# Windowed attention with a two-layer feed-forward: a list schedule, with and without 400 trial changes of its deadlines

## The chip, the cores and the metric

The kernel runs on one core of a Trainium2 chip. The metric is the device time of one execution in microseconds (us), lower is better; a profiled execution also has a span, from its first instruction to its last. The engines are TensorE (PE, its weight loads shown apart as PEld), VectorE (DVE), ScalarE (ACT), GpSimd (POOL) and SyncE (SP), which here issues every DMA of the kernel.

## The reference

```
q, k, v: [8, 8, 576, 64]                      # batch, heads, sequence, head size, float32
scores = q @ k.T / sqrt(64) + slope[h] * -|i - j|     # slope[h] = 2 ** -(h + 1)
scores = where((i >= j) & (i - j < 128), scores, -1e9)
x      = softmax(scores) @ v                  # reordered to [4608 tokens, 512]
h      = x @ w_in                             # [512, 2048]
g      = h if h >= 1; 0 if h <= -1; (h + 1) ** 2 / 4 between
out    = g @ w_out                            # [2048, 512] -> [4608, 512]
```

The weights arrive as float64 and are turned into float32 on the chip.

## The kernel before, in words

The 4608 tokens are cut into nine chunks of 512. Attention runs per chunk and head (72 heads in all, two of them a pair), in blocks of 128 queries against 256 keys: scores on TensorE (lines 667 to 674), the window and the bias on VectorE (680, 683), the exponential on ScalarE (687), a scaling by the sum (698), a turn of the block (on TensorE, line 760, for heads under 28, otherwise on VectorE and through memory), triangular masks on GpSimd (708, 711, 776, 779), and the product with the values (820). The first 16 heads work in plain float32; the later ones, like the feed-forward, split every operand into a high part in a rounded format and the rest of it, and take three products (high by high, high by rest, rest by high).

The first layer sweeps eight groups of the 2048 hidden units per chunk. Chunk 0 uses the plain blocks of w_in (A11, A12, A21, A22); chunks 1 to 8 use seven products of a Strassen form (line 883), named A11, A12, S2, S3, S1, S4 and A22 on the weight side. `build` splits such a weight block into a tile and stores it to memory (d_A, d_S, line 516); `fetch` brings it back for each later chunk (w_A, w_S, line 522) into a ring of ten places. The nonlinear step and its split are lines 894 to 903, the second layer lines 915 to 917, the copies of its sums lines 922 and 923, the stores of the result line 926.

During chunk 0 the float64 weights are loaded in 32 pieces of 512 KB (`fetch_raw`, tile raw, line 426) and turned into float32 (`convert`, ScalarE lines 451 and 461, VectorE lines 456 and 464). The raw pieces, the sixteen finished tiles of w_out, six tiles of w_in that come back from memory and one tile for turning blocks share NW = 17 places in SBUF (tag w). The tag o has two places, used in turn: for w_out on its way, for some weight sums that are being split, and for results on their way out.

All of this is not emitted in program order. Each operation is a `Node` of a `Plan` with the time that it costs on each engine that could do it; a DMA costs SP 0.4 us, then its bytes at 370 GB/s behind those before it, and lands 2.8 us or more after its issue. Each node also has a deadline (`late`). `forward` simulates the engines and lets each take, whenever it is free, the ready operation with the earliest deadline; `later` sets deadlines anew by walking that order backwards from its end. `schedule` does this twelve times, keeps the order with the earliest planned end, and the instructions are written in that order. On the chip each engine runs its own instructions strictly in that order, and semaphores hold it where an operand or a place is not ready.

Of the kernel before, what the change touches and what calls it, by code (L numbers as in the profile page):

```python
# [2 lines left out]

# [6 lines left out]
F32 = mybir.dt.float32  # L10
F32R = mybir.dt.float32r
# [18 lines left out]
PRODUCTS = (("A11", "B11"), ("A12", "B21"), ("S2", "T2"), ("S3", "T3"), ("S1", "T1"), ("S4", "B22"), ("A22", "T4"))  # L30
# [26 lines left out]
class Plan:  # L57


    CROSS, SAME, BACKLOG, STRETCH, SWAP, ROUNDS = 0.09, 0.04, 4.0, 2.0, 8.0, 12  # L60

    def __init__(self):
        self.nodes, self.slots, self.turn, self.common = [], {}, {}, {}
# [87 lines left out]

    def schedule(self, engines, bandwidth):
        self.deadlines()
        best = None
        for _ in range(self.ROUNDS):
            order = self.forward(engines, bandwidth)
            end = max(n.end for n in order)
            if best is None or end < best[0]:
                best = end, order, [(n, n.eng, n.start, n.end) for n in order], \
                    [(b, b.slot) for _, bufs in self.common.values() for b in bufs]  # L160
            self.later(order)
        for n, n.eng, n.start, n.end in best[2]:
            pass
        for b, b.slot in best[3]:
            pass
        return best[1]

    def forward(self, engines, bandwidth):
        free = {e: 0.0 for e in engines}
# [127 lines left out]
def windowed_attention_then_ffn(  # L297
# [9 lines left out]
    nc = tc.nc  # L307
# [3 lines left out]
    NT, DM = out.shape  # L311
    P = 128
    NPAIR = H // 2
    NCC = DM // P
    NFC = 16
    NG = NFC // 2
# [22 lines left out]
    def buf(pool, tag, n, shape, dtype, name):  # L339
        return plan.buf(pools[pool], tag, n, shape, dtype, name)  # L340
# [6 lines left out]
    def dve(n, f, port=False):  # L347
        return {"DVE": (n * 0.00104 + 0.068, n * 0.00104 + 0.155, f, port)}

    def dve_fast(n, f):  # L350
        return {"DVE": (n * 0.00052 + 0.070, n * 0.00052 + 0.160, f, True)}

    def act(n, f, extra=0.092):
        return {"ACT": (n * 0.00083 + extra, n * 0.00083 + extra + 0.105, f, False)}

    def act_ps(n, f):
        return act(n, f, 0.05)
# [13 lines left out]
    def pe(t, f):  # L371
        return {"PE": (t, t + 0.2, f, False)}

    def dma(nbytes, f):
        return {"SP": (0.4, 2.8, f, nbytes)}

    MM = {128: 0.112, 256: 0.1192, 512: 0.2305}

# [36 lines left out]
    wi32 = w_in.bitcast(I32)  # L415
    wo32 = w_out.bitcast(I32)
    WEIGHTS = [(g, n, f) for g in range(NG) for n in (0, 1) for f in (0, 1)]
    NW = 2 * NFC + 1 - NFC

    def fetch_raw(i):  # L420
        g, n, f = WEIGHTS[i]
        r = raw[i] = plan.shared(pools["wp"], "w", NW, [P, DM, 2], I32, f"raw_{i}", lambda free: (
            all(x.slot is not None for x in raws[:i]) and
            free > sum(x.slot is None for h, x in kept if h < g)))
        raws.append(r)
        plan.op(dma(P * DM * 8, lambda: DMA.dma_start(r.t.rearrange("p f w -> p (f w)"),
                                                      (wo32 if n else wi32)[f * NG + g])), (), [r])

    def convert(i):
        g, n, f = WEIGHTS[i]  # L430
        r = raw.pop(i)
        if n == 0:
            if f == 0:
                w_of[g] = buf("xp", ("T3", "T4", "T2")[g % 3], 1, [P, 2, DM], F32, f"w_{g}")
            w, key = w_of[g], f
        else:
            w, key = buf("fp", "o", 2, [P, DM], F32, f"fo_{g}_{f}"), None
            fo[g, f] = w

        def low():  # L440
            return r.t[..., 0]

        def high():
            return r.t[..., 1]

        def o():
            return (w.t if key is None else w.t[:, key]).bitcast(I32)

        def scale_high():
            if SIGN_BY_SLOPE:  # L450
                S.activation(high().bitcast(F32), high().bitcast(F32), AF.Prelu, scale=2.0 ** -112, alpha=2.0 ** 32)  # L451
            else:
                S.mul(high().bitcast(F32), high().bitcast(F32), 2.0 ** -112)

        def shift():
            V.tensor_scalar(o(), high(), 3, None, ALU.logical_shift_left)
            if not SIGN_BY_SLOPE:
                V.scalar_tensor_tensor(o(), high(), -0x80000000, o(), ALU.bitwise_and, ALU.bitwise_or)

        plan.op(act(DM, scale_high, 0.13), [(r, 1)], [(r, 1)])  # L460
        plan.op(act(DM, lambda: S.activation(low(), low().bitcast(U32), AF.Copy, scale=2.0 ** -29), 0.13),  # L461
                [(r, 0)], [(r, 0)])
        plan.op(dve_fast(DM, shift), [(r, 1)], [(w, key)])
        plan.op(dve(DM, lambda: V.tensor_tensor(o(), o(), low(), ALU.add), True), [(r, 0), (w, key)], [(w, key)])

    def split_out(g, f):

        o = fo.pop((g, f))
        w = wo_of[f * NG + g] = plan.shared(pools["wp"], "w", NW, [P, 2, DM], F32R, f"wo_{g}_{f}", lambda free: True)
        kept.append((g, w))  # L470
# [12 lines left out]
    def unspill(g):  # L483
        w = w_of[g] = plan.shared(pools["wp"], "w", NW, [P, 2, DM], F32, f"w32_{g}", lambda free: (
            all(x.slot is not None for _, x in kept)))
        unspilled.append(w)
        d = spilled.pop(g)
        plan.op(dma(P * DM * 8, lambda: DMA.dma_start(w.t, d.t)), [d], [w])

    def operand(g, name):  # L490

        if name[0] == "A":
            w, f = w_of[g], int(name[1]) - 1
            k0 = 0 if name[2] == "1" else 2
            return w, f, lambda: w.t[:, f, k0 * P:(k0 + 2) * P].rearrange("p (c f) -> p c f", c=2)
        if (g, name) not in sums_w:
            a, alu, b = dict(S1=("A21", ALU.add, "A22"), S2=("S1", ALU.subtract, "A11"),
                             S3=("A11", ALU.subtract, "A21"), S4=("A12", ALU.subtract, "S2"))[name]
            (ab, ak, af), (bb, bk, bf) = operand(g, a), operand(g, b)
            s = buf("fp", "sw", 4, [P, 2, P], F32, f"{name}_{g}")  # L500
            plan.op(dve(2 * P, lambda: V.tensor_tensor(s.t, af(), bf(), alu), True), [(ab, ak), (bb, bk)], [s])
            sums_w[g, name] = s
        s = sums_w[g, name]
        return s, None, lambda: s.t

    def build(g, name):
        b, key, f = operand(g, name)
        if name in PLAIN or g >= NG - LATE:
            t = buf("ring", "r", 10, [P, 2, 2, P], F32R, f"b_{g}_{name}")
        else:  # L510
            t = buf("fp", "o", 2, [P, 2, 2, P], F32R, f"b_{g}_{name}")
        plan.op(rounded(2 * P, lambda: t.t[:, 0], f), [(b, key)], [(t, 0)])
        plan.op(dve(2 * P, lambda: V.tensor_tensor(t.t[:, 1], f(), t.t[:, 0].bitcast(F32), ALU.subtract), True),
                [(b, key), (t, 0)], [(t, 1)])
        d = scratch[g, name] = plan.buf(dr, f"d_{g}_{name}", 1, [P, 4 * P], F32, f"d_{g}_{name}")
        plan.op(dma(P * 2048, lambda: DMA.dma_start(d.t, t.t.bitcast(F32).rearrange("p s c f -> p (s c f)"))), [t], [d])
        return t
# [201 lines left out]
    def turn_blocks(m, z):  # L719


        if not turned:
            turned.append(plan.shared(pools["wp"], "w", NW, [P, 2, 4 * P], F32, "turned", lambda free: (
                all(x.slot is not None for _, x in kept) and all(x.slot is not None for x in unspilled))))
# [181 lines left out]
    def layer2(c, n, fc, t):  # L906
        first, last = n == 0, n == NFC - 1
        if first and t == 0:
            accs[c] = [bank(f"acc{i // 2}", 2, f"acc_{c}_{i}") for i in range(SIZES[c])]
        a = accs[c][t]  # L910
        ts = slice(t * P, (t + 1) * P)
        w, (gh, gl) = wo_of[fc], gs[c, fc]

        def f():
            T.matmul(a.t, gh.t[:, ts], w.t[:, 0], start=first, stop=False)  # L915
            T.matmul(a.t, gh.t[:, ts], w.t[:, 1], start=False, stop=False)  # L916
            T.matmul(a.t, gl.t[:, ts], w.t[:, 0], start=False, stop=last)  # L917

        plan.op(pe(3 * MM[512], f), [gh, gl, w], [a])
        if last:  # L920
            o = buf("fp", "o", 2, [P, DM], F32, f"o_{c}_{t}")
            alts = act_ps(DM, lambda: S.copy(o.t, a.t))
            alts.update(dve(DM, lambda: V.tensor_copy(o.t, a.t)))  # L923
            plan.op(alts, [a], [o])
            r = (STARTS[c] + t) * P
            plan.op(dma(P * DM * 4, lambda: DMA.dma_start(out[r:r + P, :], o.t)), [o], ())
        if t == SIZES[c] - 1:
            del gs[c, fc]
# [22 lines left out]
    at = [0]  # L951
# [134 lines left out]
    for c in range(NCHUNK):  # L1086
        steps = sweep_steps(c)
        n = len(steps)
        now, end = ready[min(c + 1, NCHUNK)], ready[min(c + 2, NCHUNK)]
# [45 lines left out]
```

## Time and profile before

| what | value |
|---|---|
| median of three runs | 963.92 us (962.33 to 966.59) |
| profiled execution | 964.71 us, span 963.0 us |
| TensorE, VectorE, ScalarE, GpSimd busy | 99%, 90%, 69%, 23% of the span |
| granted TensorE clock | 1.000 |
| moved by DMA | 227.40 MB, mean 236 GB/s |

A busy share is the mean over stages with different limits. TensorE's matmuls are pipelined and their ends modelled, so a matmul is shown longer (0.39 us for 512 columns) than its distance from the next; how much TensorE really stands still is read from starts, waits and the chain of work.

### The profile page before, as it was taken

To read this page: it belongs to the slowest core of one execution; us is meant where nothing else is said; L and a number is where in the kernel's file an instruction comes from. 1 tells how busy PE (TensorE), PEld (TensorE's weight loads), DVE (VectorE), ACT (ScalarE), POOL (GpSimd) and SP (SyncE) were. 2 spreads that over 40 slices of the span, in tenths; PEclk is the share of its full clock that TensorE was granted. 3 is DMA by queue.
4 is the path that set the end of the run, shared out by engine and by line. 5 is a ranking of instruction groups with operands and counts; after the bars stand their busy time and mean duration, and the time that the engine had idled before them with its cause. 6 is when DMAs were issued, how large, how long until landed. Compare 5 with 4: busy or idle time off the path is not lost.

```text
span 963.0 us, 19573 instructions
## 1 busy us (share of the span) xinstructions
PE 951.1 (99%) x6320; PEld 863.4 (90%) x6320; DVE 869.9 (90%) x2183; ACT 661.4 (69%) x1657; POOL 218.5 (23%) x274
## 2 busy tenths in 40 slices
PE   8999999999999999999999999999999999999998
PEld 7889998999889998999899989899899999989987
DVE  6999999999999999999999999999999999984453
ACT  7998777877887677665876577667766777553322
POOL 2311111222331222322232212312232222210000
PEclk9999999999999999999999999999999999999999
DMA  9678886676867876887788869787888778766651
GB/s 345 235 244 276 300 269 204 229 220 222 246 204 255 253 243 211 284 259 245 223 278 254 255 212 279 244 255 223 257 276 251 218 233 272 225 174 201 174 152 44
DMA packets 133237, 227.40 MB, mean 236 GB/s; under 512 B 13712, under 2 KB 36240, under 8 KB 133136
## 3 DMA queue, kind: packets, MB, share of 16 engines
q1 hardware_dynamic: 133136, 226.15, 74.7%
q8 instruction: 51, 0.84, 0.3%
q14 instruction: 50, 0.41, 0.1%
HBM read 185.20 MB, written 40.89 MB: 235 GB/s over the span
## 4 chain that ended last, share of the span: by engine, by line
PE 83%; DVE 7%; ACT 6%; DMA 3%; issue 1%; POOL 0%; SPq 0%; ACTq 0%; DVEq 0%; POOLq 0%
PE hA L883 17%; PE hB L883 13%; PE acc L916 12%; PE acc L915 12%; PE acc L917 12%; PE x L820 6%; PE h L883 3%; PE s L673 2%; PE s L674 2%; ACT z L687 2%; PE s L671 1%; ACT raw L451 1%; DMA raw<-in_moe_w_out_dram 1%; PE p L760 1%; ACT raw L461 1%
## 5 line engine op out<-in xcount | busy, mean ns | idle before, releaser
L915 PE MATMUL acc<-wo,gh 128*128 128x512 f32 x576 | 228.0, 396 | 0.1
L916 PE MATMUL acc<-wo,gh 128*128 128x512 f32 x576 | 227.3, 395 | 0.0
L917 PE MATMUL acc<-wo,gl 128*128 128x512 f32 x576 | 225.7, 392 | 0.2
L708 POOL TENSOR_SCALAR_AFFINE_SELECT lu<-lu 128x512 fp32r<-128x512 f32 x112 | 100.6, 898 | 516.5 <-ACT lu L364 179.6
L1025 ACT COPY s<-hA 128x256 f32<-128x256 f32 x192 | 70.8, 369 | 98.7 <-PE hA L883 93.5
L687 ACT ACTIVATE z<-z,nmax 128x128 f32<-128x128 f32 x288 | 113.3, 395 | 26.9 <-DVE nmax L683 25.6
L917 PEld LDWEIGHTS acc<-wo,gl 128*128 128x128 f32 x576 | 108.2, 188 | 25.6 <-DVE gl L903 1.4
L915 PEld LDWEIGHTS acc<-wo,gh 128*128 128x128 f32 x576 | 108.9, 189 | 9.8 <-DVE o L923 0.3
L916 PEld LDWEIGHTS acc<-wo,gh 128*128 128x128 f32 x576 | 109.1, 189 | 8.8
L897 ACT ACTIVATE m<-m 128x512 f32<-128x512 f32 x144 | 90.6, 630 | 28.2 <-DVE m L894 26.3
L899 DVE SCALAR_TENSOR_TENSOR h<-h,m 128x512 f32<-128x512 f32 x128 | 95.0, 743 | 12.3 <-ACT m L897 11.7
L883 PEld LDWEIGHTS hA<-x_T,w_S 128*128 128x128 f32 x696 | 95.4, 190 | 8.7 <-ACT s L1025 3.1
L883 PE MATMUL hA<-x_T,w_S 128*128 128x256 f32 x696 | 102.2, 283 | 1.0 <-ACT s L1025 1.0
L1020 DVE TENSOR_TENSOR h<-hB,s 128x256 f32<-128x256 f32 x192 | 79.7, 415 | 24.8 <-PE hB L883 20.6
L903 DVE TENSOR_TENSOR gl<-h,gh 128x512 fp32r<-128x512 f32 x128 | 91.2, 713 | 1.9 <-ACT gh L364 0.7
L711 POOL TENSOR_SCALAR_AFFINE_SELECT lu<-lu 128x512 fp32r<-128x512 f32 x112 | 92.9, 851 | 0.0
L683 DVE CUSTOM_DVE_ANT_0 z<-s,rel 128x128 f32<-128x128 f32 x288 | 70.8, 282 | 0.5
L680 DVE COPY_PREDICATED s<-older,s 128x256 f32<-128x256 uint32 x144 | 59.8, 420 | 9.4 <-PE s L671 5.1
L364 ACT CAST gh<-h 128x512 fp32r<-128x512 f32 x75 | 46.5, 620 | 24.9 <-DVE h L899 24.0
L820 PE MATMUL x<-lu,vs 128*128 128x256 f32 (+3 forms) x560 | 62.8, 259 | 0.0
L820 PEld LDWEIGHTS x<-lu,vs 128*128 128x128 f32 (+1 forms) x560 | 57.4, 163 | 3.9 <-issue 0.2
L673 PE MATMUL s<-kk,ql 128*128 128x256 f32 x224 | 57.7, 281 | 1.0 <-DVE ql L598 0.7
(129 smaller groups left out, 2049.2 us busy)
## 6 DMA issues: line engine op xcount, KB each, us to landing
w_S<-d_S SPq DMA_DIRECT2D x232, 256.0 KB, 3.4
w_A<-d_A SPq DMA_DIRECT2D x192, 256.0 KB, 3.7
kr<-in_k_dram SPq DMA_DIRECT2D x112, 160.0 KB, 3.6
d_turn<-turned SPq DMA_DIRECT2D x44, 256.0 KB, 3.5
turned<-d_turn SPq DMA_DIRECT2D x44, 256.0 KB, 3.7
vn<-in_v_dram SPq DMA_DIRECT2D x33, 320.0 KB, 3.7
out_dram<-o SPq DMA_DIRECT2D x36, 256.0 KB, 4.1
qr<-in_q_dram SPq DMA_DIRECT2D x33, 256.0 KB, 4.2
```

The lines of the kernel that those rows point to most:

```text
L687: plan.op({"ACT": (0.385, 0.48, lambda i=i: S.activation(z.t[:, i], z.t[:, i], AF.Exp, bias=nmax.t[:, i:i + 1], scale=-1.0, accum_out=sm.t ...
L708: G.affine_select(out=lu[s].t[:, 0:2 * nb:2], in_=a.bitcast(F32), pattern=[[0, nb], [-1, P]], base=0, channel_multiplier=1, compare_op=ALU ...
L711: G.affine_select(out=a, in_=a.bitcast(F32), pattern=[[0, nb], [1, P]], base=0, channel_multiplier=-1, compare_op=ALU.is_ge, fill=0.0)
L820: T.matmul(px[:rows, q0 * P:q1 * P], sv, mv.rearrange("p a w -> p (a w)"), start=(w == 0), stop=(w == len(todo) - 1), skip_group_check=True)
L883: T.matmul(o.t[:, at:at + 2 * P], w.t[:, a, kb], x.t[:, b, kb], start=start and n == 0, stop=stop and n == len(todo) - 1, skip_group_check ...
L897: plan.op(act_fn(n, lambda: S.activation(m.t, m.t, AF.Square, scale=0.5)), [m], [m])
L899: plan.op(dve(n, lambda: V.scalar_tensor_tensor(f.t, h.t, 1.0, m.t, ALU.max, ALU.min), not psum), src + [m], dst)
L903: plan.op(dve(n, lambda: V.tensor_tensor(gl.t, f.t, gh.t.bitcast(F32), ALU.subtract), True), dst + [gh], [gl])
L915: T.matmul(a.t, gh.t[:, ts], w.t[:, 0], start=first, stop=False)
L916: T.matmul(a.t, gh.t[:, ts], w.t[:, 1], start=False, stop=False)
L917: T.matmul(a.t, gl.t[:, ts], w.t[:, 0], start=False, stop=last)
L1020: plan.op(dve(2 * P, lambda: V.tensor_tensor(f.t[:, key * 2 * P:(key + 1) * 2 * P], b.t[:, :2 * P], s.t, ALU.add)), [b, s], [(f, key)])
```

## The change

The plan tries 400 more orders behind the twelve rounds. Each takes the best order's deadlines, picks a stretch of the planned time (5, 20 or 60 us long; for even trials it begins in the first 0.3 of the span, for odd ones anywhere) and an engine, moves the deadlines of that engine's operations there by random amounts (each by its own, all of a kind by the same, or all by the same), simulates, and keeps the new order where its planned end is no later. The draws have a fixed seed. The number of places under tag w goes from 17 to 20, and that under tag o from two to four; the scratch reserved for DMAs that software issues is set to 1024. In the plan a raw load lands 4.3 us after its issue in place of 2.8. `build` no longer stores a block that none of the seven products uses (A21, eight tiles).

```diff
-    CROSS, SAME, BACKLOG, STRETCH, SWAP, ROUNDS = 0.09, 0.04, 4.0, 2.0, 8.0, 12
+    CROSS, SAME, BACKLOG, STRETCH, SWAP, ROUNDS, TRIALS = 0.09, 0.04, 4.0, 2.0, 8.0, 12, 400
...
-        best = None
-        for _ in range(self.ROUNDS):
+        best, draw = None, random.Random(1)
+        for trial in range(self.ROUNDS + self.TRIALS):
+            if trial >= self.ROUNDS:
+                self.shift(best, draw, trial)
+            late = {n: n.late for n in self.nodes}
             order = self.forward(engines, bandwidth)
             end = max(n.end for n in order)
-            if best is None or end < best[0]:
+            if best is None or end <= best[0]:
                 best = end, order, [(n, n.eng, n.start, n.end) for n in order], \
-                    [(b, b.slot) for _, bufs in self.common.values() for b in bufs]
-            self.later(order)
+                    [(b, b.slot) for _, bufs in self.common.values() for b in bufs], late
+            if trial < self.ROUNDS:
+                self.later(order)
...
+    def shift(self, best, draw, trial):
+
+        end, _, placed, _, late = best
+        for n in self.nodes:
+            n.late = late[n]
+        at, span = draw.uniform(0, end if trial % 2 else 0.3 * end), draw.choice((5, 20, 60))
+        by, kind, eng = draw.choice((0.3, 1.0, 3.0)), draw.randrange(3), draw.choice(("PE", "DVE", "DVE", "ACT", "ACT", "SP"))
+        alike, together = {}, draw.gauss(0, by)
+        for n, _, start, _ in placed:
+            if at <= start < at + span and next(iter(n.alts)) == eng:
+                if kind == 0:
+                    n.late += draw.gauss(0, by)
+                elif kind == 1:
+                    n.late += alike.setdefault(n.alts[eng][2].__code__, draw.gauss(0, by))
+                else:
+                    n.late += together
...
-        return {"SP": (0.4, 2.8, f, nbytes)}
+        return {"SP": (0.4, landing, f, nbytes)}        # landing=2.8, and 4.3 for raw loads
...
-    NW = 2 * NFC + 1 - NFC
+    NW = NFC + 4
...
-            w, key = buf("fp", "o", 2, [P, DM], F32, f"fo_{g}_{f}"), None
+            w, key = buf("fp", "o", 4, [P, DM], F32, f"fo_{g}_{f}"), None
...
+        if all(name != w for w, _ in PRODUCTS):
+            return t
         d = scratch[g, name] = plan.buf(dr, f"d_{g}_{name}", 1, [P, 4 * P], F32, f"d_{g}_{name}")
...
-    nc = bacc.Bacc("TRN2", target_bir_lowering=False, num_devices=1)
+    nc = bacc.Bacc("TRN2", target_bir_lowering=False, num_devices=1, dynamic_dma_scratch_size=1024)
```

More of the change, by code (lines that the diff above doesn't have):

```diff
@@ L1 @@
 import heapq
+import random
 from contextlib import ExitStack
@@ L372, in pe, with dma @@
         return {"PE": (t, t + 0.2, f, False)}
-    def dma(nbytes, f):
-        return {"SP": (0.4, 2.8, f, nbytes)}
+    def dma(nbytes, f, landing=2.8):
+        return {"SP": (0.4, landing, f, nbytes)}
     MM = {128: 0.112, 256: 0.1192, 512: 0.2305}
@@ L426, in fetch_raw @@
         plan.op(dma(P * DM * 8, lambda: DMA.dma_start(r.t.rearrange("p f w -> p (f w)"),
-                                                      (wo32 if n else wi32)[f * NG + g])), (), [r])
+                                                      (wo32 if n else wi32)[f * NG + g]), 4.3), (), [r])
     def convert(i):
@@ L510, in build @@
         else:
-            t = buf("fp", "o", 2, [P, 2, 2, P], F32R, f"b_{g}_{name}")
+            t = buf("fp", "o", 4, [P, 2, 2, P], F32R, f"b_{g}_{name}")
         plan.op(rounded(2 * P, lambda: t.t[:, 0], f), [(b, key)], [(t, 0)])
@@ L920, in layer2 @@
         if last:
-            o = buf("fp", "o", 2, [P, DM], F32, f"o_{c}_{t}")
+            o = buf("fp", "o", 4, [P, DM], F32, f"o_{c}_{t}")
             alts = act_ps(DM, lambda: S.copy(o.t, a.t))
```

## The prediction

> **What bounds the kernel now.** I read the page's busy times first, then the stretches, the chain of work in order of time, and last what TensorE waited for.
>
> ```profile
> span 963.0 us, 19573 instructions
> PE 951.1 (99%) x6320; PEld 863.4 (90%) x6320; DVE 869.9 (90%) x2183; ACT 661.4 (69%) x1657; POOL 218.5 (23%) x274
> ...
> 0.00:24.00 24.00, 21.38 (x122) 18.87 (x123) 16.42 (x82) 17.22 (x56) 6.01 (x25) 1.00 0.94 345
> 24.00:72.00 48.00, 44.73 (x321) 40.72 (x320) 45.84 (x149) 47.13 (x128) 11.84 (x16) 1.00 0.69 241
> 72.00:144.00 72.00, 72.00 (x481) 66.06 (x480) 69.54 (x176) 56.35 (x127) 9.67 (x10) 1.00 0.84 280
> 144.00:280.00 136.00, 134.50 (x916) 122.22 (x915) 132.54 (x350) 104.91 (x263) 33.85 (x40) 1.00 0.70 219
> 280.00:700.00 420.00, 419.19 (x2813) 380.99 (x2812) 404.95 (x985) 297.69 (x757) 114.83 (x132) 1.00 0.81 249
> 700.00:900.00 200.00, 200.00 (x1330) 182.15 (x1329) 173.31 (x393) 121.99 (x298) 42.34 (x52) 1.00 0.75 230
> 900.00:963.00 63.00, 59.32 (x351) 52.35 (x349) 27.26 (x53) 16.16 (x34) 0.00 (x0) 1.00 0.39 113
> ```
>
> The stretches give, after their length, busy us of PE, PEld, DVE, ACT, POOL, then the granted clock (1.00 throughout), the DMA share and GB/s. TensorE's idle time is 2.62, 3.27, 0, 1.50, 0.81, 0 and 3.68 us: nearly all lies in the first 72 us, between 144 and 280, and at the very end. A matmul's shown end is modelled, so busy time hides part of a stall. What the work takes by itself comes from the chain in order of time (start, us, what):
>
> ```profile
> 1.66 3.68 PE idle L1072 x16
> ...
> 64.98 1.43 PE h L883 x12
> 67.81 1.79 PE x L820 x16
> 71.03 0.86 PE s L671 x4
> 73.32 0.44 PE p L760 x4
> 161.39 0.12 PE s L674
> 163.99 0.97 PE x L820 x10
> 370.49 0.23 PE acc L915
> 371.19 0.23 PE acc L915
> 373.25 0.71 PE hB L883 x6
> ```
>
> and, from the timeline, the last matmul:
>
> ```profile
> 958.93 0.39 PE L917 MATMUL acc<-wo,gl 128*128 128x512 f32 x1
> ```
>
> The sum by these rates, counts from the code. The second layer has 9 chunks x 16 x 4 x 3 = 1728 matmuls; 370.49 to 371.19 is three of them (0.233 each), 371.19 to 373.25 nine (0.229); at 0.231 they take 399.2 us. 512 products of six at 0.715 (half of 1.43): 366.1. Values of 56 later heads at 0.965: 54.0; of the early heads, 8 with seven products and 8 with eight at 1.79/8: 26.9. Scores of later heads, 448 x 0.118: 52.9; of early heads, 32 groups at 0.86: 27.5. Transposes of 28 heads at 0.44: 12.3. The filler at the start 3.7. Together 942.6. Of the span of 963.0 this leaves 20.4: 1.7 before the first matmul, 3.8 behind the last (963.0 less 958.93 and 0.23), and about **14.9 us of stalls** strung through the run; the visible idle time without the two ends (11.88 less 1.66 and 3.68) is 6.5. So no order of this work is worth more than 15 us, and the visible part is 6.5.
>
> What TensorE's weight loads waited for in the first 72 us (total, times, longest):
>
> ```profile
> PEld s L671 <- DVE gh L774: 1.3, 1, 1.3
> PEld s L671 <- DVE xn L829: 1.3, 2, 1.0
> PEld s L671 <- ACT gh L773: 0.9, 2, 0.5
> PEld p L760 <- ACT z L687: 0.9, 2, 0.7
> PEld h L883 <- DVE x_B L854: 0.8, 1, 0.8
> PEld p L760 <- DVE z L698: 0.8, 1, 0.8
> ```
>
> With five smaller ones (0.6 to 0.2, together 2.1) and without the wait for the filler's operand at the start these are 8.1 us, and nearly every one is VectorE or ScalarE coming late with a piece of early attention: a question of order. From 24 to 72 us, VectorE is busy 45.84 and ScalarE 47.13 of 48 us, so both together have 3.0 us left there; only bringing forward what feeds more TensorE work can fill the gaps.
>
> **The change part by part.** *The trials.* They add no instruction. Even trials start their stretch in the first 0.3 of the planned end, odd ones anywhere, so about two thirds of 400 fall where the stalls are. Bounds: nothing (the planned end falls, the chip does not follow) and 8.1 us in the first 72. Durations there are steady (a group of scores 0.86, a transpose group 0.44), so a planned order can hold on the chip; but with 3.0 us of room on two engines I take less than half, 3.2 us. Behind 72 us the idle time that counts is 1.50 + 0.81 = 2.3, scattered; the plan sees perhaps a third of it, as it has no late landings: 0.8. Below nothing is possible too, since an order that the plan thinks tight has less to spare; I charge 0.3 for new stalls. If those gaps close, next in line is VectorE: 132.54 of 136 us from 144 to 280.
>
> *Buffers.* Twenty places of raw weights for 17, and four output buffers for two:
>
> ```profile
> raw<-in_moe_w_in_dram SPq DMA_DIRECT2D x16, 512.0 KB, 6.1
> raw<-in_moe_w_out_dram SPq DMA_DIRECT2D x16, 512.0 KB, 6.5
> ACT raw L451 <- DMA raw<-in_moe_w_in_dram: 2.7, 4, 1.0
> ACT raw L451 <- DMA raw<-in_moe_w_out_dram: 0.4, 1, 0.4
> ...
> ACT o L922 <- DMA out_dram<-o: 1.8, 2, 1.4
> PEld acc L915 <- DVE o L923: 0.3, 1, 0.3
> ```
>
> The whole price of late raw weights is 3.1 us on ScalarE, which stands idle 15.65 of 72 us in 72 to 144, and no row of TensorE names them there. The output buffers cost ScalarE 1.8 and TensorE 0.3. Bounds 0 and 3.4, both from these rows; the one TensorE row decides, so 0.2. Memory for them comes from the scratch of software-made DMAs, which this kernel does not issue: 0.
>
> *The longer landing* for raw loads (4.3 for 2.8 in the plan) moves them earlier in SP's order. With 512 KB at the plan's 370 GB/s (1.4 us) and 0.2, the plan expected 4.4 us and now expects 5.9, against 6.1 and 6.5 on the chip: nearer. Thirteen of the 32 loads are issued in or just behind the stretch where the DMA share is 0.94:
>
> ```profile
> 11.58 0.91 SPq L426 DMA_DIRECT2D raw<-in_moe_w_in_dram  x2
> ...
> 27.08 0.33 SPq L426 DMA_DIRECT2D raw<-in_moe_w_in_dram  x1
> ```
>
> Behind a raw load that goes early, the queries and keys wait 1.4 us of transfer each. Bounds +1.4 and -0.4 us; I take 0, as ScalarE is not late there on more than the 3.1 above. The Trainium skill, "DMA: Bandwidth & Descriptors", section "Anatomy of one DMA — SWDGE (gpsimd) path", fits 2.0 us plus bytes over 436 GB/s, an estimate of 3.2 us for 512 KB (its fit is for another path of issue); by it the loads were planned late enough before, the change only pulls them forward without need, and this term would be up to the +1.4. The rows disagree with it (6.1 and 6.5), so it gets no place in the sum.
>
> *Stores left out.* A21's eight split tiles are no longer written to memory:
>
> ```profile
> d_A<-b_A SPq DMA_DIRECT2D x32, 256.0 KB, 3.8
> L516 SPq DMA_DIRECT2D d_A<-b_A x32: 319/326/1617, 40.5 to 145.9; - x32
> ```
>
> Eight of the 32 stores go: 8 x 0.33 = 2.6 us of SP and 2.1 MB, and with each the wait for its tile at the head of SP's queue, which held back the fetches behind. No row shows TensorE waiting for a fetch, so that is 0 on the path (bounds 0 and 2.6); the room is cover for the raw loads.
>
> **Sum.** -3.2 -0.8 +0.3 -0.2 = -3.9 us. The profiled execution took 964.7 (span 963.0 and 1.7 around it), 0.8 above the median of the three runs, 963.9. So 960.8 against the profiled one and **960.0** on the median's scale. About 0.5% (4.8 us) is what a measurement of this kernel can tell from no change.
>
> **Rivals.** *A, the forecast:* a good part of the early stalls goes; 957 to 962.5. Chance 0.50.
>
> *B, the plan's gain is not the chip's:* the end improves in the plan, while the chip's remaining stalls (14.9 by the sum, of which only 8.1 stand in a place where order is plainly at fault) just move. For it: both engines that feed TensorE are nearly full from 24 to 280 us (VectorE 45.84 + 69.54 + 132.54 = 247.9 of 256). 962.5 to 966; chance 0.23.
>
> *C, most stalls go:* 8.1 at the start and 2.3 later: 963.9 - 10.4 = 953.5; 950 to 957. For it: 400 trials that never give back a gain, two thirds of them on the first 0.3. Against it: the first heads' path from load through scores, exponential, transpose and values has to be run through once before there is other work, and the 3.0 us of room. Chance 0.20.
>
> *D, slower:* fetched weights become late. The order chosen for the plan's end lets fetches of w_A and w_S come just in time by a fixed landing, while
>
> ```profile
> w_A<-d_A SPq DMA_DIRECT2D x192, 256.0 KB, 3.7
> DMA to landing us min/median/max: 2.0/3.7/7.0
> ```
>
> (last row: of all transfers from and to d_A). One at the long end is 7.0 - 3.7 = 3.3 us late, TensorE runs in order, and nothing covers it. One such fetch eats most of the gain; from three on (9.9 against 4.2 gained) the kernel is over 5 us slower, about 969. Against it: no row of TensorE's waits today names a fetch. 966 to 972; chance 0.07.
>
> **How the numbers follow.** Faster by over 0.5% means under 959.1: all of C and (959.1 - 957)/5.5 = 0.38 of A, 0.20 + 0.19 = 0.39. Slower by over 0.5% is over 968.7: most of D, 0.05. The rest, 0.56, is no change. The range 955.5 to 965.0 leaves out some 0.09 of C, 0.04 of B and all of D, 0.20; the likeliest case's own range is 957 to 962.5.
>
> **What would show it.** Right: TensorE's idle time from 0 to 72 us falls from 5.9 to about 3.5, the weight loads' waits there from 8.1 to about 5; the stretch from 280 to 900 us stays as it is; raw's waits on ScalarE and o's on TensorE vanish with the time hardly touched; d_A has 24 stores. Wrong: the early waits keep their total (B), or vanish (C), or rows of TensorE name w_A or w_S fetches as what ended a wait (D). A gain that lies behind 144 us instead would mean that I had misplaced what the trials can reach.

## The result: 5 us slower, and the profile after

The changed kernel takes 969.17 us (median of six, 967.54 to 971.97) against 963.98 for the kernel before on the same chip: a ratio of 1.0054, 95% interval 1.0041 to 1.0068. The forecast was 960.0, with 955.5 to 965.0 as its range: wrong in sign and outside the range. The plan's own end, which the program works out on the way, had gone the other way:

```
                                  before    changed
end of the order in the plan      959.08     953.70
span of the profiled execution    963.0      969.1
```

The page's head and the stretches of the changed kernel, columns as before:

```profile
span 969.1 us, 19492 instructions
PE 951.4 (98%) x6320; PEld 862.4 (89%) x6320; DVE 864.7 (89%) x2167; ACT 671.4 (69%) x1667; POOL 216.2 (22%) x274
...
0.00:24.00 24.00, 20.13 (x120) 17.87 (x121) 16.49 (x79) 17.36 (x56) 6.66 (x25) 1.00 0.93 334
24.00:72.00 48.00, 44.38 (x323) 40.90 (x323) 42.74 (x152) 47.53 (x130) 10.42 (x16) 1.00 0.75 260
72.00:144.00 72.00, 72.00 (x478) 65.97 (x477) 71.12 (x182) 60.26 (x139) 9.19 (x10) 1.00 0.80 261
144.00:280.00 136.00, 135.59 (x925) 123.49 (x924) 132.76 (x348) 102.79 (x258) 31.00 (x40) 1.00 0.67 211
280.00:700.00 420.00, 415.39 (x2783) 376.79 (x2782) 398.09 (x960) 297.89 (x743) 112.53 (x132) 1.00 0.80 247
700.00:900.00 200.00, 198.41 (x1316) 179.55 (x1315) 172.94 (x394) 127.69 (x311) 46.37 (x52) 1.00 0.75 228
```

The work is the same: TensorE is busy 951.4 us, 951.1 before, at a clock of 1.00. Its idle time is 3.87 + 3.62 in the first 72 us (5.89 before), 0.41 from 144 to 280 (1.50), and 4.61 + 1.59 = **6.2 us from 280 to 900, where it was 0.81**. The loss lies in the part that showed almost no idle time before; at the start, where I looked for the gain, the idle time grew by 1.6.

A matmul's shown end is modelled, so idle time shows only part of a stall. The distance from one matmul's start to the next shows all of it. With each kind of matmul at its median distance over all the traces here, the 6320 of them take 944.2 us, and what is left over is 13.3 us before and 19.5 after: 8.7 and 9.0 in the first 72 us, 2.4 and 1.0 from 72 to 280, 2.6 and 9.9 from 280 to 900. By this measure, called stalls by starts below, the first 72 us are about level and the loss from 280 to 900 us is 7.3.

What TensorE's weight loads waited for from 280 to 900 us, in the changed kernel:

```profile
PEld hB L907 <- DVE h L1044: 7.0, 12, 1.2
PEld hA L907 <- ACT s L1049: 5.3, 10, 1.0
```

and before:

```profile
PEld hA L883 <- ACT s L1025: 3.1, 10, 0.7
PEld hB L883 <- DVE h L1020: 1.5, 7, 0.2
```

Weight loads run ahead of the matmuls, so such a wait costs TensorE only in part. What the matmuls themselves waited for on these two, changed kernel first, then before:

```profile
PE hB L907 <- DVE h L1044: 3.5, 6, 1.0
PE hA L907 <- ACT s L1049: 1.6, 3, 0.6
```

```profile
PE hA L883 <- ACT s L1025: 0.6, 2, 0.3
```

These are the copies and additions that free the first layer's two PSUM banks. The stall below shows one such operation late because its engine was held up earlier in its list. What the operations on the turned blocks waited for, changed kernel first, then before:

```profile
DMA turned<-d_turn: 15.4, 11
```

```profile
DMA turned<-d_turn: 1.3, 4
```

One such stall from start to end, in the changed kernel's chain of work (start, us, what):

```profile
340.39 4.45 DMA turned<-d_turn
...
344.96 0.43 DVE lu L387
...
345.52 1.11 DVE lu L773
...
346.72 0.57 DVE xn L858
347.30 0.34 DVE h L1044
...
347.68 0.98 PE hB L907 x6
```

VectorE's next operation is the cast of a turned block, whose transfer lands 4.45 us after its issue. VectorE runs its list in order, so the addition that TensorE needs, some places behind, comes only at 347.30. The timeline has the same two places with the idle time ahead of them and what ended it:

```profile
344.96 0.43 DVE L387 CAST lu<-turned 128x512 fp32r<-128x512 f32 x1 [1.43 <-DMA turned<-d_turn]
...
347.68 0.98 PE L907 MATMUL hB<-x_T,w_S 128*128 128x256 f32 x6 [0.88 <-DVE h L1044]
```

VectorE lost 1.43 us to the landing, TensorE 0.88.

### The profile page after: what moved, and what is told of

The parts are those of the page before. It is cut to its first block, busy times and chain, and to the rows that moved or that the text cites. A ratio compares the mean times of both kernels' runs of the same rounds, so it can differ in the third digit from the quotient of the medians.

```text
span 969.1 us, 19492 instructions
## 1 busy us (share of the span) xinstructions
PE 951.4 (98%) x6320; PEld 862.4 (89%) x6320; DVE 864.7 (89%) x2167; ACT 671.4 (69%) x1667; POOL 216.2 (22%) x274
## 4 chain that ended last, share of the span: by engine, by line
PE 70%; DVE 12%; DMA 8%; ACT 7%; issue 2%; POOL 1%; SPq 0%; POOLq 0%; DVEq 0%; ACTq 0%
PE hA L907 14%; PE hB L907 11%; PE acc L940 10%; PE acc L939 10%; PE acc L941 10%; PE x L844 5%; PE h L907 4%; DMA turned<-d_turn 3%; DMA d_turn<-turned 2%; PE s L697 2%; ACT z L711 2%; PE s L698 2%; DVE gl L927 1%; DVE h L923 1%; PE s L695 1%
## 5 line engine op out<-in xcount | busy, mean ns | idle before, releaser
L711 ACT ACTIVATE z<-z,nmax 128x128 f32<-128x128 f32 x288 | 113.4, 395 | 19.4 <-DVE nmax L707 18.4
L923 DVE SCALAR_TENSOR_TENSOR h<-h,m 128x512 f32<-128x512 f32 x128 | 91.1, 712 | 9.8 <-ACT m L921 9.1
L735 POOL TENSOR_SCALAR_AFFINE_SELECT lu<-lu 128x512 fp32r<-128x512 f32 x112 | 93.5, 857 | 0.0
L919 ACT ACTIVATE m<-h,one 128x512 f32<-128x512 f32 x78 | 56.0, 719 | 18.6 <-DVE h L1044 9.2
```

The lines of the kernel that those rows point to most:

```text
L711: plan.op({"ACT": (0.385, 0.48, lambda i=i: S.activation(z.t[:, i], z.t[:, i], AF.Exp, bias=nmax.t[:, i:i + 1], scale=-1.0, accum_out=sm.t ...
L735: G.affine_select(out=a, in_=a.bitcast(F32), pattern=[[0, nb], [1, P]], base=0, channel_multiplier=-1, compare_op=ALU.is_ge, fill=0.0)
L923: plan.op(dve(n, lambda: V.scalar_tensor_tensor(f.t, h.t, 1.0, m.t, ALU.max, ALU.min), not psum), src + [m], dst)
```

## Experiments

Each is timed beside the kernel before on the same chip (its median there is 964.1 to 964.7; e9 to e12 ran on another chip than the rest), so ratios are what is compared. "Idle" is TensorE's from 280 to 900 us, 620 less its busy time there; "turned" is what the readers of turned blocks waited in all; the planned end is the plan's own. e12 also has another seed (2) and keeps a trial only where its score is strictly better.

| kernel | ties | planned end | time, us | ratio (95%) | idle | turned |
|---|---|---|---|---|---|---|
| before | - | 959.08 | 963.98 | 1 | 0.81 | 1.3 |
| changed | kept | 953.70 | 969.17 | 1.0054 (1.0041, 1.0068) | 6.19 | 15.4 |
| e1 no trials | - | 955.15 | 965.85 | 1.0016 (1.0007, 1.0026) | 2.99 | 7.1 |
| e2 strict | left | 953.63 | 963.13 | 0.9987 (0.9978, 0.9996) | 1.90 | 6.6 |
| e3 trials alone | kept | 955.39 | 969.78 | 1.0055 (1.0041, 1.0069) | 5.99 | 11.4 |
| e4 turned block lands later in the plan | kept | 955.91 | 968.99 | 1.0050 (1.0037, 1.0062) | 6.12 | 0 |
| e5 only equal ends | only | 955.15 | 969.48 | 1.0049 (1.0032, 1.0067) | 5.61 | 17.5 |
| e6 other seed | kept | 953.60 | 967.17 | 1.0028 (1.0016, 1.0040) | 5.70 | 18.4 |
| e7 = e2 + e4 | left | 955.42 | 964.67 | 1.0003 (0.9995, 1.0011) | 4.30 | 0 |
| e8 margin score | score | 956.16 | 965.25 | 1.0006 (0.9997, 1.0015) | 3.74 | 0 |
| e9 true prices | kept | 954.09 | 961.73 | 0.9976 (0.9963, 0.9990) | 3.92 | 5.9 |
| e10 strict, other seed | left | 953.41 | 963.36 | 0.9994 (0.9980, 1.0007) | 1.30 | 5.8 |
| e11 places alone | - | 958.19 | 967.06 | 1.0023 (1.0013, 1.0033) | 2.01 | 6.7 |
| e12 replay score | score | 953.54 | 962.37 | 0.9978 (0.9968, 0.9987) | 2.13 | 9.4 |
| **e13 strict, true prices** | left | 955.90 | **959.41** | **0.9938 (0.9922, 0.9954)** | 2.24 | 4.0 |
| e14 true prices, other seed | kept | 957.77 | 964.61 | 0.9997 (0.9987, 1.0008) | 4.52 | 10.2 |
| e15 trials alone, strict | left | 955.01 | 964.51 | 0.9996 (0.9986, 1.0007) | 3.32 | 8.8 |

The theory formed on the traces: in the changed kernel's plan TensorE has 8 us of gaps in the first 72 us and 0.3 in all the rest, so nearly any change of order behind the start leaves the planned end as it is. Of the 400 trials 301 were kept, 293 of them with exactly the same end and 8 with an earlier one. Of the 293, 154 left the order of every engine as it was; the other 139 are a random walk through orders that the plan calls equally good. The theory is that most such orders are less forgiving than the one the walk starts from: turned blocks with a reader that the plan starts within 0.3 us of the earliest time it allows behind the landing are 6 of 44 before, 8 without trials, 18 in the changed kernel. This count alone does not set the time: it is 10 in e13, the fastest kernel here.

**e1, no trials** (`TRIALS` 400 to 0).

> The changed kernel without the 400 trials; places, output buffers, longer landing and the left-out stores stay. Theory T (the trials keep nearly every order whose planned end is equal, and each such step takes away time by which operands come early; where the chip lands a transfer later than planned, ScalarE and VectorE stop in order and TensorE behind them): most of the loss goes, 960 to 964 us. Theory U (places, buffers and landing put the whole schedule in another, worse order; the trials hardly matter): as the changed kernel, 967 to 971. Theory V (any search for an earlier planned end costs margin, ties or not): 960 to 964 as well; it parts from T at the next kernel. The wait of ScalarE and VectorE for the turned block (15.4 us in the changed kernel, 1.3 before): under 4 us by T and V, about 15 by U.

965.85, 3.3 below the changed kernel but 1.6 above before, and 1.9 over the range of T and V. Most of the loss goes with the trials; theory U is out as the main cause, but the interval leaves a loss of 0.07 to 0.26% for the rest of the change. The wait of 7.1 is more than I expected.

**e2, strict**, the same trials, only strictly earlier ends kept:

```diff
-            if best is None or end <= best[0]:
+            if best is None or end < best[0]:
```

> The changed kernel with a trial kept only where its planned end is strictly earlier. T: no drift through equal ends, so the early gain stays and the margin too: 958 to 963. U: 967 to 971. V: 965 to 969, as the end is tuned just as far (the plan's own ends are within 0.1 us of each other).

963.13, 0.1 over T's range and just faster than before, with a planned end 0.07 us from that of the changed kernel. One character is worth 6 us, and V, for which it is the search for an early end that costs, falls. The stretches from 280 to 900 us of the changed kernel, e1 and e2 in this order:

```profile
280.00:900.00 620.00, 613.81 (x4097) 556.34 (x4096) 571.03 (x1352) 425.58 (x1053) 158.90 (x184) 1.00 0.79 241
```

```profile
280.00:900.00 620.00, 617.01 (x4121) 560.34 (x4120) 574.42 (x1364) 420.22 (x1041) 153.76 (x184) 1.00 0.79 241
```

```profile
280.00:900.00 620.00, 618.10 (x4126) 561.20 (x4125) 574.51 (x1358) 420.93 (x1045) 152.04 (x184) 1.00 0.79 242
```

**e3, trials alone** on the kernel before, and **e15**, the same with `<`:

> The kernel before with the 400 trials and nothing else. T: the same loss of margin from another start: 964 to 970 though the plan's end falls by 3.7 us. U: the trials help alone, 958 to 962. V: 964 to 970.

> The kernel before with the 400 trials, strictly earlier ends only (e3 without its ties). T: well below e3's 969.78, 961 to 965. If the trials cost on the old places with or without ties (two output buffers, whose readers wait for a store to land): 967 to 970, which would limit T to the new places.

969.78 and 964.51: ties cost 5.3 us from the other start too, with two output buffers and 17 places. Strict trials there gain nothing over before, though the plan promised 4.1 us.

**e5, only equal ends** kept, so that the plan gains nothing and only drifts:

```diff
-            if best is None or end <= best[0]:
+            if best is None or (end < best[0] - 1e-6 if trial < self.ROUNDS else abs(end - best[0]) < 1e-6):
```

> As the changed kernel, but a trial is kept only where the planned end stays exactly equal, so the planned end is that of the kernel without trials (955.15) and nothing but drift is added to it. T: 968 to 972, as slow as the changed kernel or slower, with the wait for the turned block again over 10 us. If it is the chase for an earlier end that costs (V): as without trials, 964.5 to 967.

969.48 with the planned end of e1: the drift alone costs 3.6 us (3.2 by the ratios), and the intervals of e1 and e5 do not meet. Its row, and what its readers of turned blocks waited for:

```profile
280.00:900.00 620.00, 614.39 (x4099) 557.29 (x4098) 572.67 (x1354) 427.60 (x1059) 146.04 (x184) 1.00 0.78 241
```

```profile
DMA turned<-d_turn: 17.5, 14
```

**e6 and e10, other seeds**, ties kept and left out (`random.Random(2)`, and `<` with `random.Random(3)`):

> The changed kernel with another seed of its draws (ties kept). T: 966 to 971, whatever the draws. If the loss was the luck of one draw (L): anywhere from 960 to 971, and under 964 in about half of such seeds.

> As e2 (strictly earlier ends only) with another seed. T: 961.5 to 965, below no trials (965.85) and below every kernel that keeps ties (967.2 to 969.8). If e2 was a lucky draw: anywhere from 962 to 970.

967.17 and 963.36. The size of the loss varies with the draw, its sign does not: the four kernels with ties at the plan's own prices and landings (changed, e3, e5, e6) are at 1.0028 to 1.0055 with 5.6 to 6.2 us idle; the three with strict trials (e2, e10, e15) at 0.9987 to 0.9996 with 1.3 to 3.3. Stalls by starts from 280 to 900 us are 9.2 to 9.9 in those four, 5.4 without trials (e1) and 2.4 to 5.9 in the three strict ones.

The margin in the plan goes the same way. The measure that e8 below scores adds up how much each TensorE group behind 72 us lacks of starting 1 us after its operands. Taken of the plans, it is 90 us without trials (e1), 94 and 85 with strict trials (e2, e10), and 128, 120 and 115 with ties (changed, e5, e6). From the kernel before, with 82, strict trials come to 100 (e15) and ties to 111 (e3). So ties do spend margin; these are planned times, and that the missing margin is what the chip pays for is the theory.

**e4, the turned block lands later in the plan** (4.3 us in `turn_blocks` for both transfers), ties kept; **e7** with strict trials; **e8** with a score:

```diff
+            score = end + self.EARLY * self.tight(order)   # 0.1 us per us by which a TensorE group starts under 1 us after its operands
```

> The changed kernel, in whose plan the two transfers of a turned block land 4.3 us after issue in place of 2.8 (trials and ties as they are). If the margin is lost above all at the readers of the turned block (T in its narrow form): the waits for it fall from 15.4 to under 4 us and the time to 959 to 964. If the drift takes margin everywhere alike: 964 to 968. U: 967 to 971.

> Strictly earlier ends only, and 4.3 us landing for the two transfers of a turned block in the plan. T: margin is kept as in e2 and no reader waits for the turned block (6.6 us there): 958 to 962, with the first 72 us as in e4 (TensorE busy 67.8 of 72 there against 65.0 in e2). L: 963 to 969, as e4.

> As e7, but an order is scored by its planned end plus 0.1 us for every us by which a matmul group behind 72 us starts less than 1 us after its operands. T: better than e7 where margin is what counts, 956 to 961. If margin in the plan does not say how the chip runs: as e7 or slower, 961 to 967.

968.99, 964.67, 965.25. The waits for turned blocks vanish in e4, and its time does not care; by itself it lies where U put it, which e2 has ruled out. So my narrow reading was wrong, and the wide one (964 to 968) misses by 1 us. The margin lacking in its plan is 128 us, as in the changed kernel: the turned block is where the eroded margin showed, not where it must show. In e4 the same two waits stand without it (from 280 to 900 us):

```profile
PEld hB L907 <- DVE h L1044: 5.7, 11, 1.1
PEld hA L907 <- ACT s L1049: 4.3, 7, 1.0
```

e7 missed its 958 to 962 and lies where L put it. e8, for which margin as the plan sees it is the aim, is no better, but it is a weak test: its plan lacks 93.5 us of margin against 99.8 in e7 and 93.8 in e2, so the score moved little of it. What the margin of a plan says of the chip stays open here. The next question was the plan's prices.

**e9, true prices.** From one start to the next on a full VectorE, the plan's price for nearly every operation agrees with the trace (0.60 us for 512 columns). Two do not: the turn of 32x32 blocks takes 1.03 where the plan has 0.600, and the low part of the queries, half of the partitions into the other half, 0.717 for 0.600. Their rows in the changed kernel, with an ordinary operation of the same length last (mean ns of one behind the comma, which includes the end of the pipe):

```profile
L753 DVE STREAM_TRANSPOSE turned<-z 128x512 f32<-128x512 f32 x44 | 48.6, 1104 | 0.4 <-DMA d_turn<-turned 0.2
L622 DVE SCALAR_TENSOR_TENSOR ql<-qr,ql 64x512 fp32r<-64x512 f32 x56 | 40.7, 726 | 1.7
L927 DVE TENSOR_TENSOR gl<-g,gh 128x512 fp32r<-128x512 f32 x16 | 11.4, 710 | 0.0
```

That is 44 x 0.43 + 56 x 0.117 = 25 us of VectorE which the plan did not know of.

```diff
-        plan.op(dve(4 * P, block, True), [z], [(t, 0)])
+        plan.op({"DVE": (1.03, 1.12, block, True)}, [z], [(t, 0)])
...
-            plan.op(dve(n, lo, True), [(b, key), (ql, (j, 0))], [(ql, (j, 1))])
+            plan.op({"DVE": (0.717, 0.80, lo, True)}, [(b, key), (ql, (j, 0))], [(ql, (j, 1))])
```

> The changed kernel, ties kept, with VectorE's two underpriced operations at what the trace shows from start to start: the 32x32 turn 1.03 us in place of 0.600 (44 times), the low part of the queries 0.717 in place of 0.600 (56 times), 25 us of VectorE in all. Theory P (orders look tight but possible only because the plan gives VectorE 25 us too little work; true prices cure it, ties or not): 958 to 963. Theory T (late landings against an eroded margin): 965 to 970, hardly better than the changed kernel.

> As e9 (true prices, ties kept) with another seed, whose planned end is 3.7 us later (957.77 against 954.09). P: 960 to 965, still below every kernel that keeps ties at the plan's own prices. If e9 was a lucky draw (L): 965 to 970.

961.73 with ties kept, faster than before; with another seed 964.61, no different from before. Both lie where P put them and below every kernel that keeps ties at the old prices; T's 965 to 970 for e9 is missed. But idle time from 280 to 900 is still 3.92 and 4.52 (by starts 6.4 and 7.0, against 5.4 in e1), and e14's readers of turned blocks wait 10.2 us, so prices do not cure the drift; e9's gain over before is at the start, as the next run shows.

**e13, true prices and strict trials:**

> True prices of the two VectorE operations (as e9) and strictly earlier ends only (as e2). If ties cost margin at any price (T): TensorE's stalls from 280 to 900 us fall from e9's 7.5 to about 5, 958 to 962. If prices alone decide (P): as e9 within 1 us, with the same stalls there.

959.41, 0.6% below before (0.9938, 0.9922 to 0.9954): faster than both kernels and in the range of T; P, for which ties do not matter at true prices, is out on this seed, though ties cost only 2.3 us here (e9 against e13). e9 (first row and third) against e13 (second and fourth):

```profile
0.00:72.00 72.00, 69.00 (x475) 63.33 (x476) 62.63 (x232) 67.02 (x192) 20.12 (x42) 1.00 0.81 287
```

```profile
0.00:72.00 72.00, 68.13 (x475) 62.90 (x476) 63.19 (x230) 66.81 (x193) 20.31 (x42) 1.00 0.81 291
```

```profile
280.00:900.00 620.00, 616.08 (x4113) 560.38 (x4112) 560.54 (x1321) 434.42 (x1075) 145.50 (x180) 1.00 0.79 241
```

```profile
280.00:900.00 620.00, 617.76 (x4131) 563.42 (x4130) 563.49 (x1337) 431.98 (x1063) 145.76 (x180) 1.00 0.79 242
```

In the first 72 us both have 475 matmuls on TensorE and 3.0 and 3.9 us idle; the kernel before has 5.9 idle there and some 441 matmuls (122 and 321, less those on the cut). Against the changed kernel TensorE's idle time falls by 3.6 at the start and 4.0 behind 280. The plan also moves work to ScalarE, which has room: 432 us there for 426. Idle time hides most of e13's gain over before. By starts, the first 72 us have 3.7 us of stalls in e13 and 3.8 in e9, 8.7 before: 5.0 of the 5.1 us that e13 gains in span. From 280 to 900 us e13 has 3.1, e9 6.4, before 2.6. (The 7.5 in the expectation is reckoned with medians of that trace alone; reckoned so, e13 has 4.9, as T had it.)

**e11, places alone** (no trials, raw loads at 2.8 us again), and **e12**, whose score is the mean end of six replays of an order with transfers that land up to 1.5 us late:

> No trials, and the plan's landing of raw loads back at 2.8 us: of the change only the places, the output buffers and the left-out stores stay. If these cost nothing and the longer landing gave the 1.6 us that e1 is slower than before: 962.5 to 964.5. If any new order at all loses some margin of the order before: 965 to 968.

> The changed kernel with another score for a trial: not the planned end but the mean end of six replays of its order, in which every engine runs its list in order, each transfer lands 0.5 us earlier to 1.5 us later than planned at random, and the two underpriced operations take their traced time; kept only where strictly better. T: the fastest of all, 957 to 962, and the waits for the turned block under 5 us. If such a replay misses what holds the chip up: 962 to 966, as e2.

967.06, slower than before by 0.13 to 0.33%: the places, buffers and left-out stores alone put the schedule into another order with worse stalls. With the longer landing (e1) the ratio is 1.0016 for 1.0023, but the two intervals overlap (1.0007 to 1.0026, 1.0013 to 1.0033), so what the landing does is not told apart from nothing. e12 at 962.37 is faster than before but just misses T's range, and the waits for turned blocks are 9.4 and not under 5: such a replay sees only part of what holds the chip up. It is still 4.8 us below e6, which has the same seed and keeps ties by the planned end.

## Why the prediction was wrong, point by point

*What bounds the kernel:* held. Work and clock did not change, and every kernel here has the same 6320 matmuls and differs by its stalls alone. The 14.9 us of stalls that the sum left over are 13.3 by starts.

*The trials, -3.2 us in the first 72 us:* failed. That stretch went from 5.9 to 7.5 us idle (by starts from 8.7 to 9.0), and the weight loads' waits there from 8.1 to 9.0, the largest of them now

```profile
PEld p L784 <- ACT gh L797: 1.6, 1, 1.6
PEld s L695 <- ACT lu L797: 1.2, 2, 0.9
PEld s L691 <- PE s L695: 1.2, 1, 1.2
```

The early stalls are a question of order, as I said: e13 and e9 got 2.0 and 2.9 us of idle time back (5.0 and 4.9 by starts), and so did e4 at the old prices (1.7 and 4.7). But this run of trials did not find it, and the plan already says so: TensorE's gaps in the first 72 us fall there from 8.7 to 8.2 us only. The two thirds of the trials that I counted on fall in the first 290 us; 79 began in the first 72, and three of these found an earlier end, 0.7 us together. Of the plan's gain of 5.4 us the trials brought only 1.4 (955.15 in e1 to 953.70).

*-0.8 behind 72 us:* right up to 280 us (1.50 to 0.41).

*+0.3 for new stalls:* this is the step that decided. It measured +5.4 us of idle time from 280 to 900 (0.81 to 6.2), 7.3 by starts. The prediction names the mechanism, an order that the plan thinks tight and that has less to spare, but gives it 0.3 with no row behind the number. It ties the new stalls to an earlier end; that a trial is kept "where its planned end is no later", so that margin can go while the end stands still, did not enter the sum. The rows were there: from 280 to 900 us TensorE stood idle for 0.81 us, so the plan had next to nothing to gain. Of the 127 trials that began in that stretch none found an earlier end, 115 were kept as ties, and 55 of those changed the order.

*Buffers, -0.2:* their own effects came as written. ScalarE's wait for raw weights fell from 3.1 to 0.7, the waits for output stores are gone, d_A has 24 stores. Yet e11, which also leaves out the stores, is slower than before by 0.13 to 0.33%, some 2 us: the edit gave another order, and that was not in my bounds.

*The longer landing, 0:* nothing in e1 against e11 speaks against it. The loads land in

```profile
raw<-in_moe_w_in_dram SPq DMA_DIRECT2D x16, 512.0 KB, 5.7
raw<-in_moe_w_out_dram SPq DMA_DIRECT2D x16, 512.0 KB, 5.9
d_A<-b_A SPq DMA_DIRECT2D x24, 256.0 KB, 4.3
```

which is the 5.9 that the plan now expects. The Trainium skill's fit ("DMA: Bandwidth & Descriptors", "Anatomy of one DMA — SWDGE (gpsimd) path") would give an estimate of 3.2, for another path of issue; the trace disagrees with it here, and the loads it would have called needlessly early cost nothing that shows.

*Rival D* had the right mechanism in the wrong place: transfers that land late against an order with nothing to spare, in-order engines behind them, 966 to 972. I put it at the fetched weights and gave it 0.07, since no row of TensorE named a fetch. No row does now either. The late transfer sits one engine further back, before ScalarE and VectorE, and reaches TensorE as a late copy or addition.

*The chances:* the range leaves out more than the 0.20 given. Spread evenly, as A was, C has 0.16 below 955.5 and B 0.07 above 965.0; with D that is 0.29.

*Left open:* how much of the loss is late landings and how much underpriced VectorE work. e4 has no wait for turned blocks and is as slow, e9 and e14 have true prices and about two thirds of the idle time left; no run removes both causes with the drift kept. A calculation points to the landings: e12's replay, applied to the finished orders, lengthens the changed kernel's by 9.7 us and e2's by 4.4 with late transfers alone, either by 0.3 with true prices alone, and by 13.3 and 5.4 with both. It is a hint and no more, since the same replay ends the kernel before (965.8) almost as late as the changed one (966.5). Nor was it tried which of the two prices matters.

## What to carry to other kernels

When a planner accepts changes that leave its objective equal, ask what the objective does not see: here slack. The 293 ties, 139 of them real changes of order, cost 3.6 to 6 us on a kernel whose plan said 5.4 us faster. Accept strictly better only (or score what the plan cannot see), and check the plan's price of every operation against start-to-start distances in a trace before searching further. For a forecast, compare the planned end with the measured span of the same order first; when a search moves the plan only where TensorE is already full, expect the chip to get nothing for it, and bound the new stalls by more than a token.

## What the runs showed of the hardware

A 32x32-block turn on VectorE of 128x512 floats occupies it for about 1.03 us from start to start, where other operations of that length take 0.60 (duration 1104 ns against 710 as a mean). The transfer of a turned block back from memory, 256 KB, lands in 3.8 us as a median of 44 in the changed kernel and can take 5.59, as in its chain:

```profile
412.04 5.59 DMA turned<-d_turn
```
